# Block-wise search of the early gates, separate buffers for the last router step, a new work list, and the expert stage written once per arm of the branch

## The chip, the cores and the metric

The kernel runs on one core of a Trainium2 chip. The metric is the device time of one execution in microseconds (us), as a median over runs. The core's engines are TensorE (PE, with its weight loads shown as PEld), VectorE (DVE), ScalarE (ACT), GpSimd (POOL) and SyncE (SP). Each works through its own instructions in the order in which they stand, and they wait for each other through semaphores. SP does no arithmetic here; it issues the bulk transfers.

## The reference

A gated linear recurrence over time gives 20224 tokens of 256 numbers, and a mixture of eight experts with a capacity of 80 tokens each works on them. The `x` of the second part is the `h` of the first for four sequences of S = 5056 steps, `gate_w` is the softmax value of the chosen expert. Only the tokens with the highest gates of each expert get an output; all other rows of the output are zero.

```python
log_a = c * sig_r * np.log(np.clip(a_base, 1e-06, 1.0 - 1e-06))[None, None, :]
a_t = np.exp(log_a)
norm = np.sqrt(np.maximum(1.0 - a_t * a_t, 1e-06))
x_gated = norm * sig_i * x
for t in range(S):
    h = a_t[:, t] * h + x_gated[:, t]
...
logits = x @ w_gate
expert_idx = np.argmax(logits, axis=1)
...
for e in range(E):
    tok_idx = np.where(expert_idx == e)[0]
    if len(tok_idx) > capacity:
        keep = np.argpartition(-gate_w[tok_idx], capacity)[:capacity]
        tok_idx = tok_idx[keep]
    h = np.maximum(x[tok_idx] @ w1[e], 0.0)
    out[tok_idx] = gate_w[tok_idx, None] * (h @ w2[e])
```

## The kernel before

**Stage one, the recurrence and the router.** The tokens are cut into 40 units of 512 (the last has 256). For each unit SP loads `r`, `i` and `x` (`load`, L116) into slots of one big tile `Y`; the table `SLOTS` says which. PE transposes `r` (L124), ACT takes its tanh (L126) and the decay `a` (`decay`, L138), POOL squares `a` (`square`, L141), ACT takes a root (`root`, L144) and the tanh of `i` (`i_tanh`, L148). POOL (`u` in the list, L152 and L153) or DVE (`v`, L155) multiplies by `x`, PE transposes the product (L160), DVE applies the norm (`normed`, L163) and runs the recurrence as a scan (`scan`, L171). Some steps take two units at once (`e0.2` is the decay of units 0 and 1). Four finished units make a group. `logits` (L233) multiplies a group by the router's weights into the PSUM tile `pl`, and ten short steps (`stages`) turn two groups into gates: copy (L237), turn by PE (L241), maximum (L252, L253), exp (L258), first maximum (L262 to L264), sum on POOL (L269 to L272), reciprocal (L275), gate (L278), turn back (L283), store into `rows` (L287). There is one `pl` and one `lg` for all steps. `rows` then holds, on each of 128 partitions (16 token classes by 8 experts), the gates of 1264 tokens.

**What sets the order.** `ORDER` is a list of tokens, written out by hand, which fixes the order on ACT, PE, DVE and POOL. SP's order is left to the scheduler. `Z` is one zero fill of the output (256 tokens, 256 KB, L218), of which 79 are needed; fills that the list doesn't hold come after it.

**Selection.** `early_top` (`T`, L292 to L297) searches the first eight groups (1024 columns of `rows`) for the 16 largest per partition after the last scan, while the last router step runs. `top16` then searches those 16 and the last 240 columns together (256 columns). From there DVE, POOL, ACT and PE work out each candidate's rank among the partitions of its expert (`others`, `columns`, `place`, `parts`) and pick the 80 places per expert with matmuls into `sel`, copied to `chosen` (L429). Fourteen candidates per partition are enough in the usual case; if they are not for some partition, `flag` is positive, and `general` (L431 to L473) does it with 80.

**The branch.** PE and DVE load `flag` (L474) and compare (L476). `general` lies right behind the branch, some 480 instructions on DVE and 86 on PE. A hint for the branch is issued on both engines. The program's common rest lies behind `general`; ACT, POOL and SP go to it without looking at `flag`.

**Expert stage.** PE turns `chosen` into columns (L483), DVE makes them integers (L486), and ACT, POOL and DVE each load some columns of an expert into registers (`fetch`, L499) and copy those tokens (L505, L506) into `XG`. PE runs both layers (`products`, L520 and L522), DVE and ACT the relu, DVE the weighting (L530), POOL the scatter (L533). SP loads the weights (L320, L323) of experts 0 and 1 ahead of the last 34 fills, and those of a later expert when its buffers are free. L588 is the program's end, with its barrier.

Of the kernel before, what the change touches and what calls it, by code (L numbers as in the profile page):

```python
# [24 lines left out]
STEPS = ((0, 1), (2, 3), (4, 5), (6, 7), (8, 9))  # L25
SLOTS = dict(r=(1, 2, 3, 4, 5, 10, 14, 16, 21, 22, 13, 24, 29, 31, 33, 27, 37, 38, 41, 21, 22, 35, 44, 45, 46, 30, 40, 48, 31, 33, 49, 43, 36, 46, 47, 44, 49, 43, 42, 47),
             i=(6, 8, 9, 19, 20, 9, 19, 27, 30, 20, 32, 34, 18, 19, 23, 20, 40, 34, 43, 32, 36, 24, 27, 33, 42, 32, 36, 47, 34, 44, 32, 41, 40, 48, 42, 45, 37, 46, 45, 48),
             x=(11, 13, 15, 8, 11, 23, 25, 15, 26, 28, 35, 36, 30, 25, 26, 18, 42, 28, 47, 29, 48, 25, 26, 43, 28, 38, 41, 29, 42, 45, 38, 34, 35, 41, 38, 40, 48, 41, 40, 44),
             a=(0, 7, 12, 17, 18, 6, 7, 8, 12, 9, 11, 17, 14, 15, 16, 19, 23, 17, 20, 31, 49, 34, 23, 37, 24, 25, 27, 35, 28, 37, 30, 31, 32, 33, 34, 35, 36, 38, 41, 39))
# [50 lines left out]
def moe_kernel(ctx, tc, x, r_gate, i_gate, a_param, w_gate, w1, w2, out, capacity=80):  # L80
# [142 lines left out]
    def width(g): return min(512, (N - 2048 * g) // 4)  # L223
    def logits(g):

        s = plan.step_of[g]; k = g - plan.steps[s][0]; last = g == plan.steps[s][-1]
# [366 lines left out]
```

## Time and profile before

| | us |
|---|---|
| median of 3 runs | 332.15 (331.56 to 332.41) |
| the profiled execution, its own time | 329.29 |
| its span in the trace | 327.5 |

Of the span the engines are busy for 68% (PE and DVE) and 71% (ACT and POOL). The last scan ends at 225.4 us. The first matmul of the expert stage starts at 264.65 us, and the rest of the span is the expert stage. Busy times and waits are read per stretch, since the three stages have different limits. A line's rows name what it writes and reads (out<-in), the shape, and the number of instructions.

### The profile page before, as it was taken

The page shows a single profiled execution, that of the slowest core. Times are in us where ns is not written, and L with a number is a line of the kernel's source. Part 1 is how long each engine was busy: PE and PEld are TensorE (multiplying, and loading weights), DVE is VectorE, ACT ScalarE, POOL GpSimd, SP SyncE. Part 2 cuts the span into 40 slices and gives each one's busy share as a digit, 9 for nine tenths or more (in the row PEclk, how much of TensorE's full clock was granted, in tenths as well). Part 3 has the DMA queues.
Part 4 walks back from the last instruction along what each step waited for, and adds up shares of the span by engine and source line. Part 5 has one row for each costly group of instructions (what it writes and reads, how often), then busy time and mean ns, then how long its engine had stood idle before and what let it go on. Part 6 is the DMA issues. An engine that isn't in the chain of part 4 may idle for free. (4 is left out here: it accounts for less than half of the span.)

```text
span 327.5 us, 5668 instructions
## 1 busy us (share of the span) xinstructions
PE 222.6 (68%) x1400; PEld 169.1 (52%) x1400; DVE 222.7 (68%) x515; ACT 231.2 (71%) x454; POOL 231.5 (71%) x358
## 2 busy tenths in 40 slices
PE   3663838496669855798644776348253668999994
PEld 3562833255565343754523326222142558999994
DVE  1047978968579993998659796799684174466611
ACT  6999999989969999689659998891131063453500
POOL 2494999789699999799996989981253167453712
PEclk9957678578579995599975797957757675999999
DMA  7999999999987479896996879999999942999940
GB/s 251 409 404 345 385 412 410 409 370 393 366 327 234 162 260 372 274 309 220 313 366 215 277 208 355 392 374 296 370 375 375 335 165 67 301 353 336 343 149 20
DMA packets 52532, 100.70 MB, mean 307 GB/s; under 512 B 4368, under 2 KB 32912, under 8 KB 52496
## 3 DMA queue, kind: packets, MB, share of 16 engines
q1 hardware_dynamic: 52112, 99.64, 86.0%
q0 software_dynamic: 384, 0.66, 0.6%
q8 instruction: 13, 0.21, 0.3%
q14 instruction: 23, 0.19, 0.2%
HBM read 78.91 MB, written 21.36 MB: 306 GB/s over the span
## 5 line engine op out<-in xcount | busy, mean ns | idle before, releaser
L171 DVE TENSOR_TENSOR_SCAN Y<-Y,pu 128x512 f32<-128x512 f32 (+4 forms) x86 | 97.5, 1169 | 0.4
L160 PE MATMUL pu<-ident,Y 128*128 128x128 f32 x316 | 61.2, 334 | 44.9 <-DVE Y L171 33.6
L141 POOL TENSOR_TENSOR Y<-Y 128x1024 f32<-128x1024 f32 (+2 forms) x29 | 75.2, 2608 | 16.4 <-ACT Y L138 15.9
L160 PEld LDWEIGHTS pu<-ident,Y 128*128 128x128 f32 x316 | 44.4, 172 | 68.3 <-issue 46.3
L153 POOL TENSOR_TENSOR Y<-Y 128x1024 f32<-128x1024 f32 (+2 forms) x25 | 72.9, 2916 | 2.2 <-POOL Y L152 0.2
L124 PE MATMUL pr<-ident,Y 128*128 128x128 f32 x316 | 55.9, 341 | 26.9 <-DMA Y<-in_r_gate_dram 19.0
L124 PEld LDWEIGHTS pr<-ident,Y 128*128 128x128 f32 x316 | 49.1, 181 | 32.4 <-ACT Y L126 14.1
L163 DVE SCALAR_TENSOR_TENSOR pu<-Y,pu 128x512 f32<-128x512 f32 (+1 forms) x80 | 51.2, 676 | 16.5 <-ACT Y L144 11.7
L138 ACT ACTIVATE Y<-Y,tiny 128x512 f32<-128x512 f32 (+2 forms) x58 | 52.4, 961 | 3.0 <-POOL Y L271 2.4
L520 PE MATMUL ph<-Y 128*128 128x80 f32 x256 | 45.7, 273 | 4.4 <-DMA out_dram<-Y 3.0
L522 PE MATMUL po<-Y,rows 128*80 128x128 f32 x256 | 48.3, 282 | 0.0
L148 ACT ACTIVATE Y<-Y 128x1024 f32<-128x1024 f32 (+2 forms) x29 | 38.7, 1359 | 7.8 <-DMA Y<-in_i_gate_dram 7.6
L126 ACT ACTIVATE Y<-pr 128x1024 f32<-128x1024 f32 (+1 forms) x40 | 39.1, 1005 | 7.1 <-PE pr L124 7.1
L520 PEld LDWEIGHTS ph<-Y 128*128 128x128 f32 x256 | 40.6, 206 | 5.0 <-POOL Y L506 3.4
L505 ACT COPY Y<-Y 128x2 f32 x224 | 22.8, 191 | 26.2 <-issue 23.7
L506 POOL COPY Y<-Y 128x2 f32 x192 | 24.3, 200 | 24.0 <-issue 16.1
L152 POOL TENSOR_SCALAR Y<-Y 128x1024 f32<-128x1024 f32 (+2 forms) x25 | 33.8, 1352 | 9.7 <-ACT Y L148 7.3
L233 PE MATMUL pl<-Y 128*32 128x512 f32 (+2 forms) x176 | 37.3, 986 | 2.0 <-ACT rows L287 2.0
L144 ACT ACTIVATE Y<-Y 128x1024 f32<-128x1024 f32 (+2 forms) x32 | 38.0, 1248 | 0.4 <-POOL Y L141 0.3
L522 PEld LDWEIGHTS po<-Y,rows 128*80 128x80 f32 x256 | 29.8, 158 | 0.0
L506 DVE COPY Y<-Y 128x2 f32 x224 | 24.7, 178 | 7.2 <-issue 7.0
L155 DVE SCALAR_TENSOR_TENSOR Y<-Y 128x1024 f32<-128x1024 f32 x9 | 18.0, 2002 | 17.0 <-ACT Y L148 14.8
(131 smaller groups left out, 159.5 us busy)
## 6 DMA issues: line engine op xcount, KB each, us to landing
out_dram<-Y SPq DMA_DIRECT2D x79, 256.0 KB, 4.7
Y<-in_r_gate_dram SPq DMA_DIRECT2D x39, 512.0 KB, 6.3
Y<-in_i_gate_dram SPq DMA_DIRECT2D x39, 512.0 KB, 6.8
Y<-in_x_dram SPq DMA_DIRECT2D x39, 512.0 KB, 5.8
Y<-in_moe_w_dram SPq DMA_DIRECT2D x32, 512.0 KB, 5.0
Y<-in_r_gate_dram SPq DMA_DIRECT2D x1, 256.0 KB, 7.6
Y<-in_x_dram SPq DMA_DIRECT2D x1, 256.0 KB, 7.4
Y<-in_i_gate_dram SPq DMA_DIRECT2D x1, 256.0 KB, 5.2
```

What stands on the lines that cost most here:

```text
L124: nc.tensor.transpose(pr[:, h, b:nb * P:nb], rr[:, b, h * P:(h + 1) * P], ident)
L126: nc.scalar.activation(rslot(u), prs.pop(u)[:, :, :ntok(u)], AF.Tanh, scale=0.5)
L138: nc.scalar.activation(a[:, :, h], z[:, :, h], AF.Exp, scale=L[:, h:h + 1], bias=L[:, h:h + 1])
L141: nc.gpsimd.tensor_tensor(pair('r', u, m), a, a, op=ALU.mult)
L148: nc.scalar.activation(i, i, AF.Tanh, scale=0.5)
L153: nc.gpsimd.tensor_tensor(v, i, v, op=ALU.mult)
L160: nc.tensor.transpose(pu[:, b:nb * P:nb], tmb('x', u)[:, b, h * P:(h + 1) * P], ident)
L163: nc.vector.scalar_tensor_tensor(pu, rslot(u)[:, h], 0.5e-3, pu, op0=ALU.max, op1=ALU.mult)
L171: nc.vector.tensor_tensor_scan(y[:, s0:s1], a[:, s0:s1], q[:, s0:s1], init, op0=ALU.mult, op1=ALU.add)
L506: else: eng.tensor_copy(dst, src)
L520: nc.tensor.matmul(ph[:, c % (FC // 2)], w1v(e1)[:, h, c * P:c * P + P], XG[:, e1, h], start=(h == 0), stop=(h == 1))
L522: nc.tensor.matmul(po[:, h, :P], h2T[:, c], w2v(e2)[:, c, h * P:h * P + P], start=(c == 0), stop=(c == FC - 1))
```

## The change

- **Early search by blocks.** `T` is gone. `P0` to `P3` (`cell_top`) each search 256 columns of `rows` for the eight largest, once these are stored, in the midst of stage one. `M0` to `M2` (`merge`) find the 16 largest of these 32 (DVE) and their columns (DVE, then POOL with a product and halving sums). The eighth of each block, in `eighth`, guards the result: `full` is zero for a candidate that isn't above it, and `fl` counts the candidates that are both out of reach of the capacity and above it, so that `flag` stays zero only if the blocks' eight were enough.
- **Router.** The last two groups are steps of their own: `STEPS` is now `((0, 1), (2, 3), (4, 5), (6, 7), (8,), (9,))`. The last step has its own PSUM tile (a buffer of `ps_r`), its own slot of `Y` in place of `lg`, and its own small columns. Its logits come in two parts: `Ga` for three units, `Gb` for the last; its sum and its gate are on DVE.
- **Work list.** `SLOTS` and `ORDER` are new in every row. Units with the product on DVE are 11 (before 9), on POOL 29 (before 31); pairs are 10, 10, 6 and 10 for decay, square, root and tanh of `i` (before 11, 11, 8 and 11). The weights of experts 0 and 1 (`W0` to `W7`) are in the list. Of the fills 63 are in the list (before 45).
- **Branch.** All five engines load `flag` and compare. The usual arm, a whole copy of the expert stage, stands right behind the comparison; the other arm holds `general` and a second copy. The hints are gone. At its end the usual arm jumps over the other: 975 instructions on DVE, 474 on ACT, 418 on POOL, 390 on PE, 48 on SP.

```diff
-STEPS = ((0, 1), (2, 3), (4, 5), (6, 7), (8, 9))
+STEPS = ((0, 1), (2, 3), (4, 5), (6, 7), (8,), (9,))
...
+    s39.1 xg38.0 W3 R4.0 Tu39.0 xg38.1 R4.1 y38.0 Z W4 y38.1 Tu39.1 Z R4.2 Ga Z xg39.0 R4.3 xg39.1 y39.0 Z y39.1 W5 R4.4 R4.5 Gb Ca M0 W6 R5.0 R5.1
+    W7 R5.2 M1 Z R4.6 R5.3 R5.4 Z Z R5.5 R4.7 R5.6 M2 R4.8 Z R5.7 R5.8 Z R4.9 R5.9
...
+    def logits_first():
+        st['pl', LAST_STEP] = ps_r.tile([P, 2, C], F32, name="pr")[:, 0]
+        spread(LAST, list(range(4 * LAST, NU - 1)))
+    def logits_last(): spread(LAST, [NU - 1])
+    lgs = [lg] * LAST_STEP + [Y[:, NU + 9, 0]]
...
+        if s == LAST_STEP:
+            nc.vector.tensor_reduce(out=total[:n, NR:2 * NR], in_=ex9(n), op=ALU.add, axis=AX.X)
+            return
...
-    def early_top():
-        top16(rows[:, :NE], rows[:, NE:NE + K1], eidx, rows[:, :NE])
-        nc.vector.tensor_copy(ecol, eidx)
+    def cell_top(s):
+        src, c = rows[:, 2 * P * s:2 * P * s + 2 * P], slice(8 * s, 8 * s + 8)
+        nc.vector.max(cell[:, c], src)
+        nc.vector.max_index(cidx[:, c].bitcast(U32), cell[:, c], src)
+    def merge(n):
+        if n == 0:
+            nc.vector.tensor_reduce(out=eighth, in_=cell[:, 7:NC:8], op=ALU.max, axis=AX.X)
+            top16(cell, rows[:, NE:NE + K1], pos.bitcast(U32), cell)
+            nc.vector.tensor_tensor(where, pos.bitcast(U32).unsqueeze(2).broadcast_to([P, K1, NC]), nth.unsqueeze(1).broadcast_to([P, K1, NC]), op=ALU.is_equal)
+        pool = nc.gpsimd
+        if n == 1:
+            pool.tensor_copy(cidx, cidx.bitcast(U32))
+            by8 = cidx.rearrange("p (s k) -> p s k", k=8)
+            pool.tensor_tensor(by8, by8, cell0.unsqueeze(2).broadcast_to([P, 4, 8]), op=ALU.add)
+            pool.tensor_tensor(where, where, cidx.unsqueeze(1).broadcast_to([P, K1, NC]), op=ALU.mult)
+        if n == 2:
+            w = NC // 2
+            while w:
+                pool.tensor_tensor(ecol if w == 1 else where[:, :, :w], where[:, :, 0] if w == 1 else where[:, :, :w],
+                                   where[:, :, 1] if w == 1 else where[:, :, w:2 * w], op=ALU.add)
+                w //= 2
...
-    nc.vector.tensor_scalar(fl, rk[:, K - 1:K], float(CAP), None, op0=ALU.is_lt)
+    nc.vector.scalar_tensor_tensor(lt[:, :K], rk[:, :K], float(CAP), full[:, :K], op0=ALU.is_lt, op1=ALU.mult)
+    nc.vector.tensor_reduce(out=fl, in_=lt[:, :K], op=ALU.add, axis=AX.X)
...
-    _, fv = nc.values_load_multi_w_load_instructions(flag, engines=[E_.PE, E_.DVE], min_val=0, max_val=P,
-    with tc.If(fv[0] > 0, label="many"):
-        general(KG)
+    _, fv = nc.values_load_multi_w_load_instructions(flag, engines=[E_.PE, E_.DVE, E_.Activation, E_.Pool, E_.SP], min_val=0, max_val=P,
+    with tc.If(fv[0] < 1) as usual:
+        experts("u")
+    with usual.Else():
+        gstack = ExitStack()
+        general(KG, gstack.enter_context(tc.tile_pool(name="ps_gen", bufs=1, space=bass.MemoryType.PSUM)))
+        gstack.close()
+        experts("g")
```

On DVE, from the last scan to the last router step's gate. Before, `rows` is searched (L292 to L297) between the scan and the router step (L252 on):

```order
L171 SCALAR_TENSOR_TENSOR Y<-Y,pu 128x256 x2
L292 MAX rows<-rows 128x8
L293 MAX_INDEX tiny<-rows 128x8
L294 MATCH_REPLACE rows<-rows 128x1024
L292 MAX rows<-rows 128x8
L293 MAX_INDEX tiny<-rows 128x8
L297 CAST tiny<-tiny 128x16
L252 TENSOR_REDUCE Y<-pl 128x32
L253 TENSOR_TENSOR pl<-pl,Y 128x16x16
L262 SCALAR_TENSOR_TENSOR pl<-pl,tiny 128x16x16
```

After, in the new kernel's lines, where L283 to L285 end the step of group 8, L330 to L333 are the merge, and L268 begins the last step:

```order
L172 SCALAR_TENSOR_TENSOR Y<-Y,pu 128x256 x2
L283 SCALAR_TENSOR_TENSOR pl<-pl,tiny 128x16x8
L385 TENSOR_TENSOR lg<-lg,ident 48x16
L284 TENSOR_REDUCE Y<-pl 128x16
L285 TENSOR_TENSOR lg<-pl,Y 128x128
L330 TENSOR_REDUCE Y<-Y 128x1
L312 MAX rows<-Y 128x8
L313 MAX_INDEX Y<-rows,Y 128x8
L314 MATCH_REPLACE Y<-rows,Y 128x32
L312 MAX rows<-Y 128x8
L313 MAX_INDEX Y<-rows,Y 128x8
L333 TENSOR_TENSOR Y<-Y 128x512
```

The search over 1024 columns has left this place, and one over 32 columns with a comparison of 512 elements stands there. On POOL, from the last product of stage one on, the rows before are the sum, the gate and two constants:

```order
L153 TENSOR_TENSOR Y<-Y 128x512
L269 TENSOR_TENSOR lg<-lg 128x32x4
L270 TENSOR_TENSOR lg<-lg 128x32x2
L271 TENSOR_TENSOR Y<-lg 128x32
L272 TENSOR_SCALAR Y<-Y 128x32
L278 TENSOR_TENSOR lg<-lg,Y 128x16x2x8
L331 IOTA lg 128x128
L334 IOTA lg 128x80
```

After, L336 to L339 and L343 are the merge, L299 is the gate of group 8, and L378 makes the constant that DVE's L379 reads:

```order
L336 CAST tiny<-tiny 128x32
L338 TENSOR_TENSOR tiny<-tiny,Y 128x32
L339 TENSOR_TENSOR Y<-Y,tiny 128x512
L299 TENSOR_TENSOR lg<-lg,Y 128x128
L343 TENSOR_TENSOR Y<-Y 128x16x16
L343 TENSOR_TENSOR Y<-Y 128x16x8
L378 IOTA lg 128x128
L343 TENSOR_TENSOR Y<-Y 128x16x4
L343 TENSOR_TENSOR Y<-Y 128x16x2
L343 TENSOR_TENSOR tiny<-Y 128x16
```

The merge's products have come in front of the gate and of the constant. On SP, around the last loads of stage one, before:

```order
L116 DMA Y<-in_x_dram 128x512
L116 DMA Y<-in_i_gate_dram 128x512
L218 DMA out_dram<-Y 256x1x256 x23
L320 DMA Y<-in_moe_w_dram 128x2x512 x4
L323 DMA Y<-in_moe_w_dram 128x4x256 x4
L218 DMA out_dram<-Y 256x1x256 x8
L476 UNCONDITIONAL_BRANCH
L218 DMA out_dram<-Y 256x1x256 x26
```

After:

```order
L117 DMA Y<-in_r_gate_dram 128x512
L221 DMA out_dram<-Y 256x1x256 x5
L350 DMA Y<-in_moe_w_dram 128x2x512 x4
L221 DMA out_dram<-Y 256x1x256
L353 DMA Y<-in_moe_w_dram 128x4x256
L221 DMA out_dram<-Y 256x1x256 x3
L353 DMA Y<-in_moe_w_dram 128x4x256 x3
L221 DMA out_dram<-Y 256x1x256 x21
L522 TENSOR_LOAD lg
L615 COMPARE_AND_BRANCH
```

Behind the last load 30 fills are left (before 57), so 49 stand ahead of it (before 22); behind the last weights of experts 0 and 1 there are 21 (before 34).

## Rows read from the trace of the kernel before

**Rows 1.** The page's first part: busy time, share of the span and instructions of each engine.

```profile
PE 222.6 (68%) x1400; PEld 169.1 (52%) x1400; DVE 222.7 (68%) x515; ACT 231.2 (71%) x454; POOL 231.5 (71%) x358
```

**Rows 2.** The view by stretches, for stage one from 100 us on: stretch and length, busy us of PE, PEld, DVE, ACT and POOL with their instructions, granted TensorE clock, mean busy share of the 16 DMA engines, GB/s.

```profile
100.00:120.00 20.00, 16.97 (x110) 9.20 (x108) 19.49 (x23) 19.73 (x19) 19.83 (x8) 1.00 0.58 189
120.00:140.00 20.00, 12.04 (x52) 9.98 (x53) 14.54 (x21) 16.58 (x19) 17.91 (x12) 0.59 0.96 330
140.00:160.00 20.00, 17.04 (x110) 9.52 (x109) 16.21 (x18) 18.34 (x18) 19.68 (x9) 0.98 0.80 280
160.00:180.00 20.00, 9.36 (x51) 6.56 (x50) 16.14 (x24) 14.40 (x17) 16.55 (x13) 0.70 0.83 287
180.00:200.00 20.00, 14.17 (x77) 6.53 (x77) 17.47 (x19) 19.27 (x22) 18.71 (x12) 0.84 0.82 265
200.00:220.00 20.00, 10.01 (x55) 7.63 (x53) 15.14 (x21) 17.54 (x21) 17.33 (x15) 0.76 1.05 374
```

**Rows 3.** The view of waits, whole span: engine and line, what it waited for, us in total, times, longest us.

```profile
ACT Y L148 <- DMA Y<-in_i_gate_dram: 7.6, 3, 5.0
...
ACT Y L126 <- PE pr L124: 7.1, 7, 2.4
```

**Rows 4.** The view of instruction groups with shapes kept apart, from 0 to 226 us: count, busy us, mean ns of one, idle time before.

```profile
L153 POOL TENSOR_TENSOR Y<-Y 128x1024 f32<-128x1024 f32 x18 | 44.4, 2464 | 1.5
...
L138 ACT ACTIVATE Y<-Y,tiny 128x1024 f32<-128x1024 f32 x22 | 26.0, 1232 | 2.5 <-POOL Y L271 2.4
L138 ACT ACTIVATE Y<-Y,tiny 128x512 f32<-128x512 f32 x34 | 25.6, 807 | 0.5 <-DVE pu L163 0.3 <-POOL Y L153 0.2
L144 ACT ACTIVATE Y<-Y 128x1024 f32<-128x1024 f32 x23 | 23.1, 1047 | 0.1
L148 ACT ACTIVATE Y<-Y 128x2048 f32<-128x2048 f32 x11 | 21.0, 1905 | 0.1
L152 POOL TENSOR_SCALAR Y<-Y 128x1024 f32<-128x1024 f32 x18 | 20.8, 1155 | 7.3 <-ACT Y L148 7.3
L155 DVE SCALAR_TENSOR_TENSOR Y<-Y 128x1024 f32<-128x1024 f32 x9 | 18.0, 2002 | 17.0 <-ACT Y L148 14.8 <-DMA Y<-in_x_dram 2.2
L148 ACT ACTIVATE Y<-Y 128x1024 f32<-128x1024 f32 x17 | 17.7, 1049 | 7.7 <-DMA Y<-in_i_gate_dram 7.6
L144 ACT ACTIVATE Y<-Y 128x2048 f32<-128x2048 f32 x8 | 15.1, 1903 | 0.0
```

**Rows 5.** The timeline from the last scan to the search of 256 columns, and three later instructions of like kind: start us, us, engine and line, operation, out<-in, shape and count.

```profile
224.00 1.38 DVE L171 TENSOR_TENSOR_SCAN Y<-Y,pu 128x256 f32<-128x256 f32 x2
...
225.29 1.20 DVE L292 MAX8 rows<-rows 128x8 f32<-128x1024 f32 x1
...
231.86 0.42 DVE L252 TENSOR_REDUCE Y<-pl 128x32 f32<-128x256 f32 x1
...
233.33 0.45 POOL L269 TENSOR_TENSOR lg<-lg 128x128 f32<-128x128 f32 x1 [11.41 <-ACT lg L258]
...
235.81 0.62 POOL L278 TENSOR_TENSOR lg<-lg,Y 128x256 f32<-128x256 f32 x1 [1.03 <-DVE Y L275]
...
237.04 0.23 POOL L331 IOTA lg<- 128x128 int32 x1 [0.61 <-PE pl L283]
...
237.71 0.42 DVE L292 MAX8 lg<-rows 128x8 f32<-128x256 f32 x1
...
242.46 0.68 POOL L345 TENSOR_TENSOR Y<-Y,tiny 128x256 f32<-128x256 f32 x1
...
247.97 0.15 DVE L414 TENSOR_SCALAR lg<-lg 128x1 f32<-128x1 f32 x1
248.04 0.79 DVE L420 TENSOR_TENSOR Y<-lg 128x560 bf16<-128x560 f32 x1
```

**Rows 6.** The sequencers' load of `flag` (L474) and the branch (L476): engine, operation, count, duration in ns (least/median/most), first and last start in us.

```profile
L474 DVEq TENSOR_LOAD <-lg x1: 879/879/879, 250.5 to 250.5; - x1
...
L476 PEldq EVENT_SEMAPHORE  x1: 51/51/51, 251.2 to 251.2; - x1
L476 DVEq COMPARE_BRANCH  x1: 90/90/90, 251.5 to 251.5; - x1
L476 DVEq EVENT_SEMAPHORE  x1: 21/21/21, 255.9 to 255.9; - x1
```

**Rows 7.** The timeline around the branch, and the expert stage's first matmuls.

```profile
250.37 0.23 DVE L429 COPY lg<-sel 48x80 f32<-48x80 f32 x1 [0.71 <-PE sel L426]
...
255.98 0.43 PE L483 MATMUL pv<-lg 48*8 48x80 f32 x2 [5.72 <-DVEq L476]
...
264.65 5.05 PE L520 MATMUL ph<-Y 128*128 128x80 f32 x32 [3.01 <-DMA out_dram<-Y]
```

**Rows 8.** DVE's loads of columns into registers (L499, 28 registers each, one load per expert): columns as in rows 6. The first starts at 256.8 us.

```profile
L499 DVEq TENSOR_LOAD <-lg x8: 1848/1852/4105, 256.8 to 304.1; - x8
```

**Rows 9.** The timeline of SP's queue: the fills behind the last load of stage one, and those behind the first weights.

```profile
207.41 17.59 SPq L218 DMA_DIRECT2D out_dram<-Y  x23
...
232.37 30.01 SPq L218 DMA_DIRECT2D out_dram<-Y  x34
```

**Rows 10.** POOL's sequencer at the end of the program (L588): its drain, the longest of which begins at 323.5 us, and the barrier's semaphores. Columns as in rows 6.

```profile
L588 POOLq EVENT_SEMAPHORE  x4: 17/17/17, 326.7 to 327.4; - x4
L588 POOLq DRAIN  x3: 40/108/2906, 323.5 to 327.2; - x3
```

More of the change, by code (lines that the diff above doesn't have):

```diff
@@ L94, in moe_kernel @@
     Y = big.tile([P, NU + EXTRA, 2, C], F32, name="Y")
-    tiny = const.tile([P, 58], F32, name="tiny")
+    tiny = const.tile([P, 74], F32, name="tiny")
     ident = const.tile([P, P], F32, name="ident")
@@ L323, in load_w2, with weights @@
         nc.sync.dma_start(w2v(e)[:, c], w2[e].rearrange("(c p) d -> p c d", p=P)[:, c])
-    for e, g in ((0, 0), (0, 1), (1, 0), (1, 1)): load_w1(e, g)
-    for e, g in ((0, 0), (0, 1), (1, 0), (1, 1)): load_w2(e, g)
+    WLOADS = [(load, e, g) for load in (load_w1, load_w2) for e in range(2) for g in range(2)]
+    def weights(w):
+        load, e, g = WLOADS[w]
+        load(e, g)
+    tasks = {'Lr': lambda u: load('r', u, rf), 'Li': lambda u: load('i', u, jf), 'Lx': lambda u: load('x', u, xf),
+             'Tr': r_transposes, 'tr': r_tanh, 'e': decay, 'q': square, 's': root, 'ti': i_tanh, 'u': gated, 'v': gated,
+             'Tu': u_transposes, 'xg': normed, 'y': scan, 'G': logits, 'R': lambda s, k: stages[k](s), 'Ga': logits_first, 'Gb': logits_last, 'Ca': copy_first, 'P': cell_top, 'M': merge, 'W': weights, 'Z': lambda: zero_fill(1)}
+    with tc.manual_schedule(engines={E_.Activation, E_.PE, E_.DVE, E_.Pool}):
+        for n, (kind, *args) in enumerate(plan.order):
+            tasks[kind](*args)
+            if n == GATE_AT: nc.sync.dma_start(wg[:, :, E:2 * E], w_gate.rearrange("(h p) e -> p h e", p=P))
+    mstack.close()
+    CAP = capacity
+    assert 0 < CAP <= 80
+    tstack = ExitStack()
+    ps_t = tstack.enter_context(tc.tile_pool(name="ps_t", bufs=1, space=bass.MemoryType.PSUM))
     zero_fill(-(-N // ZERO_TOKENS))
@@ L454, in general @@
             kw = min(16, K - c0)
[L455 removed]
+            others(cv, c0, kw, bd, vv, ps_t)
             for k in range(K):
@@ L480, in moe_kernel @@
-    tail.__enter__()
-    pc = ps_t.tile([E, CAP], F32, name="pv")
-    nc.tensor.matmul(pc, comb[:3 * V, :E], chosen, start=True, stop=True)
-    col = lg[:E, :CAP].bitcast(I32)
-    nc.vector.tensor_scalar(col, pc, -1.0, 0.0, op0=ALU.add, op1=ALU.max)
-    pt = ps_t.tile([CAP, 2 * E], F32, name="sel")
-    nc.tensor.matmul(pt, chosen, comb[:3 * V], start=True, stop=True)
-    keep_warm(WARM[1])
-    flat = slot(0, NU)
-    XG = scr[:, :E * 2 * CAP].rearrange("p (e h s) -> p e h s", e=E, h=2)
```

336 lines of the change are left out of this document (177 added, 159 removed).

## The prediction

> **What bounds the kernel now.** I read the page's busy times first. No engine is above 71% of the span [rows 1], so the end is set by chains of waits, and each stage has to be read for itself.
>
> In stage one the view by stretches [rows 2] shows ACT and POOL close to full: from 100 to 120 us 19.73 and 19.83 of 20 us, from 180 to 200 us 19.27 and 18.71. ACT's idle time has named causes, among them 7.6 us for loads of `i` and 7.1 us for transposes of `r` [rows 3]. The transfers are not full there: shares of 0.58, 0.96, 0.80, 0.83 and 0.82 between 100 and 200 us leave (0.42 + 0.04 + 0.20 + 0.17 + 0.18) x 20 = 20.2 us of idle queue, and only after 200 us is the share 1.05 [rows 2].
>
> The second stage is one long chain. The last scan ends at 224.00 + 1.38 = 225.38 us. DVE then searches 1024 columns from 225.29 to about 231.8, and only then gets to the last router step (L252 at 231.86); the search over 256 columns starts at 237.71 [rows 5], 12.33 us after the scan. `chosen` is written by 250.60, but PE's next matmul starts at 255.98 [rows 7]. The sequencer view says why: DVE branches at 251.5 and its next event is at 255.9, 4.4 us later, though PE had passed the same branch at 251.2 [rows 6]. Next, the first load of columns into registers takes 4.1 us where its median is 1.85 [rows 8], and the expert stage starts at 264.65 [rows 7]. The change aims at this stretch of 39.3 us; the expert stage behind it does the same work as before.
>
> **Stage one, part by part.** The new list splits pairs on ACT. One pair of decays less and two single units more cost 4 x 0.807 - 2 x 1.232 = 0.76 us; two pairs of roots less, 4 x 1.047 - 2 x 1.903 = 0.38; one pair of tanh less, 2 x 1.049 - 1.905 = 0.19: together 1.3 us on the busiest engine [rows 4]. POOL loses two units, 2 x (1.155 + 2.464) = 7.2 us, and DVE gains them, 2 x 2.00 = 4.0 us [rows 4], and the block searches, eight instructions of about 0.42 (L292 on 256 columns, rows 5), 3.4 us. DVE is at 14.5 to 17.5 of 20 us in most stretches [rows 2], so I count that as hidden under ACT; where DVE is late the scans are late with it. Two router instructions of about 0.25 us now stand on DVE ahead of the last norm, where nothing hides them: 0.5 us. So stage one gets 1.8 us longer. I give no credit for POOL's relief: the idle times of ACT in rows 3 don't name it. Bounds: 5 us shorter, if the list removes a third of ACT's 14.7 us of waits for data [rows 3]; 8 us longer, by the fills (third rival).
>
> **The router's tail.** Let T be the end of the last scan. On DVE now follow three operations on 128 elements, which I put at 0.27 between 0.15 (a tiny one, L414) and 0.42 (256 elements, L252), with a small one of 0.16: 1.0 us. The merge: a reduction and five instructions over 32 columns at 0.2 with their overhead, 1.15 us, and the comparison of 512 elements at 0.75, just under L420's 0.79 for 560. That is T + 2.9. POOL then multiplies 512 elements (1.1 us, above L345's 0.68 for 256), gates group 8 (0.45, as L269), halves twice (0.68 and 0.45) and only then makes the constant (0.23, L331) which DVE's next instruction but three reads: T + 5.9 [all rows 5]. DVE waits there: its own last router step could have been there by T + 4.4. Two small constants at 0.23 and four operations of about 0.27 follow, T + 7.5. From the gate's end to the search before were 237.71 - (235.81 + 0.62) = 1.28 us [rows 5]; with half the columns I take 1.1. So the search over 256 columns starts at T + 8.6 in place of T + 12.33: **3.8 us gained** (5.4 if POOL's merge isn't waited for, 1.8 if every small operation costs what a 256-wide one does).
>
> **The guard.** Four more small DVE instructions up to `chosen`, at 0.15 each [rows 5], two of them where DVE waits for PE anyway: **0.3 us lost** (0 to 0.6).
>
> **The branch.** The usual arm now stands right behind the comparison, so I expect no engine to jump there. The flag's load (0.88 us) and the comparison (0.09) stay [rows 6]. DVE's 4.4 us go: **4.4 us gained** (0 to 4.7; the upper end is PE, past the branch at 251.2 and idle until 255.98, rows 6 and 7). Late next is PE itself, which then needs only `chosen`. The three engines that now also load the flag have nothing queued between it and the loads of columns. SP does: it stands behind its last fills, but what it issues in the arm (weights of expert 2) is first needed after two experts.
>
> **The first load of columns.** It takes 4.1 us at 256.8, while SP still issues fills until 232.37 + 30.01 = 262.4 [rows 8, 9]; loads later, beside weight transfers, take 1.85. That the fills slow it is my reading and not shown. A fill takes 30.01 / 34 = 0.88 us, so 13 fills fewer behind the weights end 11.5 us earlier against T, while the load itself comes 3.8 - 0.3 + 4.4 = 7.9 us earlier: the fills' end moves from 5.6 us after its start to 2.0 us after. I take half of the difference: **1.1 us gained** (0 to 2.25).
>
> **The end.** Every engine now jumps over the second arm when it is done. DVE's jump over 480 instructions cost 4.4 us [rows 6]. POOL is last; its drain begins at 323.5 and ends with the last scatter, and the barrier follows at 326.7 [rows 10]. A jump of 4.4 us from 323.5 would end at 327.9, 1.2 us late; one under 3.2 us is hidden. **0.5 us lost** (0 to 1.3), since the transfers there are nearly idle.
>
> [...]
>
> **Sum.** -3.8 + 0.3 - 4.4 - 1.1 + 0.5 + 1.8 = -6.7 us. The profiled execution took 329.29 us (span 327.5), so its like would take 322.6. The median of the three runs is 332.15, and the difference applied to it gives 325.4.
>
> **Rivals.** [...] (2) *The merge buys nothing*: the search leaves DVE, but POOL's product and halvings take its place as the wait in front of L379, with every operation at the 256-wide price and the rest slow as well; the router's term is 0, 329.2. For it: POOL stands idle there for 11.41 us before, so the work is new on the chain [rows 5]; against: the prices. (3) *Slower: the fills choke the loads.* 27 more fills stand ahead of the last load of stage one. At 17.59 / 23 = 0.76 us each [rows 9] they need 20.6 us of a queue with 20.2 us idle. Two bursts of eight and nine stand ahead of loads; each holds a load back by up to 9 x 0.76 = 6.9 us. If stage one gets 10 us longer in place of 1.8, the time is 333.6. The sign turns when the fills take more than 6.7 + 1.8 = 8.5 us from ACT. Against: the scheduler puts them where SP has no free slot to load into. (4) *Stage one gets shorter*: the list removes 5 us of ACT's waits, and its term is -3.2: 320.4.
>
> **How the numbers follow.** Forecast 325.4 with 0.55 (its own range about 321 to 329); rival 1 0.12, rival 2 0.06, rival 3 0.14, rival 4 0.13. The range from 318.0 to 332.0 leaves out most of rival 3 and the low end of rival 4, and takes in the bounds of the router (+2.0, -1.6), the branch (+4.4) and the load (+1.1, -1.1). A difference of 0.3%, about 1 us, is what a measurement here can tell from none. Faster by more: the forecast, rival 4, and nearly all of rivals 1 and 2, 0.82. Within: the overlaps of rivals 1, 2 and part of 3, 0.05. Slower: rival 3, 0.13.
>
> **What would show it.** In the new trace: from the last scan to the search over 256 columns 8.6 us in place of 12.33, with DVE's constant (L379) waiting for POOL; DVE's next event within 0.5 us of its branch; the first load of columns near 3 us, and near 1.85 if the fills are done by then, 4.1 though they are done if my reading of it is wrong; the drain at the end no more than 1.3 us longer; the last scan between 222 and 230 us. The forecast is wrong if the last scan ends after 233 us, or if an engine still stands for 4 us behind its branch.

## The result: 4% faster, twice the forecast

| | before | changed |
|---|---|---|
| median, us | 332.03 (331.56 to 332.41, 4 runs) | 318.2 (316.55 to 318.73, 4 runs) |
| profiled execution, us (span) | 329.29 (327.5) | 318.39 (316.7) |

The ratio is 0.9576, 95% interval 0.9538 to 0.9613. In the runs below the kernel before was timed 52 times beside other kernels, with medians of 330.26, 330.97, 330.44 and 329.83 us and single times from 326.9 to 333.3; the changed kernel came to 317.48 (ratio 0.9596) and 317.57 (0.9626) in two of them. So the first four runs of before were a little high, and the change is worth some 13 us. The forecast was 325.4, 6.7 us less than 332.15; the median of 318.2 lies just inside the range from 318.0 to 332.0, the two later ones just below it. Runs more than 1.5% above the fastest of their kernel (327.18, 327.63 and 320.61 us below, the second of them the first profiled execution with late fills) are in the medians, but no stage is read from them, and where they shift a comparison the median without them is given.

Three profiled executions of the changed kernel and two of before, stage by stage. Each column is the mean of the stage's length; the last is the forecast's term.

| stage, us | before | changed | difference | forecast |
|---|---|---|---|---|
| start to the end of the last scan | 226.4 (225.4, 227.4) | 224.8 (226.1, 224.6, 223.7) | -1.6 | +1.8 |
| to the search over 256 columns | 12.3 | 8.2 | -4.2 | -3.8 |
| to the end of the copy of `chosen` | 12.8 | 12.8 | 0.0 | +0.3 |
| to PE's next matmul | 5.5 | 0.5 | -5.0 | -4.4 |
| to the first expert matmul | 8.6 | 6.9 | -1.7 | -1.1 |
| to the issue of the last scatter | 58.9 | 57.2 | -1.8 | 0 |
| to the end of the span | 3.7 | 5.0 | +1.3 | +0.5 |
| sum | 328.3 | 315.4 | -12.8 | -6.7 |

The page's first part of the changed kernel, to be held against [rows 1]:

```profile
PE 215.4 (68%) x1404; PEld 162.0 (51%) x1404; DVE 228.1 (72%) x541; ACT 233.5 (74%) x463; POOL 227.9 (72%) x370
```

ACT does 2.3 us more (the count of split pairs had 1.3) and DVE 5.4 more, and yet the kernel is shorter. Three stretches of the view beside [rows 2]:

```profile
100.00:120.00 20.00, 16.95 (x106) 8.95 (x104) 19.38 (x18) 19.80 (x22) 18.30 (x8) 0.99 0.99 350
...
140.00:160.00 20.00, 15.09 (x92) 9.49 (x84) 14.76 (x17) 17.57 (x19) 19.75 (x8) 0.88 0.98 350
...
180.00:200.00 20.00, 13.88 (x84) 7.41 (x76) 17.14 (x21) 17.96 (x20) 18.57 (x12) 0.91 0.93 356
```

The DMA share, next to last, is 0.99, 0.98 and 0.93 where it was 0.58, 0.80 and 0.82: most of the idle time of the queue is gone, as 27 more fills stand ahead of the last load. ACT's waits, beside [rows 3]:

```profile
ACT Y L149 <- DMA Y<-in_i_gate_dram: 4.5, 4, 2.9
...
ACT Y L127 <- PE pr L125: 3.6, 7, 1.2
...
ACT lg L276 <- DVE pl L269: 3.2, 2, 2.5
```

The waits for `i` and for transposes of `r` fell from 14.7 to 8.1 us, though the queue is fuller. A wait for the router's maximum (L269) is new.

DVE from the last scan to the search over 256 columns, beside [rows 5]:

```profile
225.38 0.72 DVE L172 TENSOR_TENSOR_SCAN Y<-Y,pu 128x256 f32<-128x256 f32 x1
...
226.93 0.18 DVE L312 MAX8 rows<-Y 128x8 f32<-128x32 f32 x1
...
228.34 0.69 DVE L333 TENSOR_TENSOR Y<-Y 128x512 f32<-128x512 uint32 x1
...
230.30 0.29 DVE L284 TENSOR_REDUCE Y<-pr 112x16 f32<-112x128 f32 x1
232.07 0.33 DVE L379 TENSOR_SCALAR lg<-lg 128x128 int32<-128x128 int32 x1 [1.48 <-POOL lg L378]
...
234.26 0.43 DVE L312 MAX8 lg<-rows 128x8 f32<-128x256 f32 x1 [0.83 <-ACT rows L307]
```

and POOL in the same stretch:

```profile
229.17 1.09 POOL L339 TENSOR_TENSOR Y<-Y,tiny 128x512 f32<-128x512 f32 x1 [2.58 <-DVE Y L333]
230.22 0.41 POOL L299 TENSOR_TENSOR lg<-lg,Y 128x128 f32<-128x128 f32 x1
230.59 1.26 POOL L343 TENSOR_TENSOR Y<-Y 128x256 f32<-128x256 f32 x2
231.80 0.24 POOL L378 IOTA lg<- 128x128 int32 x1
```

DVE is at its last router step by 230.3 and stands for 1.48 us until POOL, which has the merge ahead of it, makes the constant (L378). The branch and PE behind it, beside [rows 6] and [rows 7], first by the sequencers' comparisons, then by PE's timeline:

```profile
L615 POOLq COMPARE_BRANCH  x2: 40/40/41, 247.5 to 311.7; - x2
L615 PEldq COMPARE_BRANCH  x2: 92/1797/3502, 247.6 to 309.0; - x2
L615 DVEq COMPARE_BRANCH  x2: 51/55/59, 247.8 to 311.1; - x2
```

```profile
247.81 0.42 PE L532 MATMUL pv<-lg 48*8 48x80 f32 x2 [1.06 <-DVE lg L476]
...
254.68 1.54 PE L569 MATMUL ph<-Y 128*128 128x80 f32 x12 [0.21 <-DVE lg L592]
```

No engine stands at the branch: PE's next matmul starts at 247.81. The second time on each of these lines is the jump over the other arm at the end. The loads of columns, beside [rows 8], and SP's fills, beside [rows 9]:

```profile
L548 DVEq TENSOR_LOAD <-lg x8: 1849/1857/1957, 248.7 to 292.2; - x8
```

```profile
211.91 3.63 SPq L221 DMA_DIRECT2D out_dram<-Y  x5
...
228.29 17.80 SPq L221 DMA_DIRECT2D out_dram<-Y  x21
```

The last fill is issued by 246.1, ahead of the first load of columns at 248.7, and none of the eight loads is slow. At the end, beside [rows 10], POOL's and DVE's sequencers:

```profile
L645 DVEq DRAIN  x2: 10/25/40, 314.1 to 316.1; - x2
L645 POOLq EVENT_SEMAPHORE  x4: 17/17/17, 315.9 to 316.6; - x4
L645 POOLq DRAIN  x3: 40/107/1262, 314.3 to 316.4; - x3
```

### The profile page after: what moved, and what is told of

The parts are those of the page before. It is cut to its first block, busy times and chain, and to the rows that moved or that the text cites. A ratio compares the mean times of both kernels' runs of the same rounds, so it can differ in the third digit from the quotient of the medians.

```text
span 316.7 us, 5713 instructions
## 1 busy us (share of the span) xinstructions
PE 215.4 (68%) x1404; PEld 162.0 (51%) x1404; DVE 228.1 (72%) x541; ACT 233.5 (74%) x463; POOL 227.9 (72%) x370
## 5 line engine op out<-in xcount | busy, mean ns | idle before, releaser
L142 POOL TENSOR_TENSOR Y<-Y 128x1024 f32<-128x1024 f32 (+2 forms) x30 | 74.2, 2487 | 26.0 <-ACT Y L139 23.6
L161 PE MATMUL pu<-ident,Y 128*128 128x128 f32 x316 | 56.4, 319 | 38.5 <-DVE Y L172 23.3
L125 PE MATMUL pr<-ident,Y 128*128 128x128 f32 x316 | 53.7, 329 | 31.5 <-DMA Y<-in_r_gate_dram 26.9
L161 PEld LDWEIGHTS pu<-ident,Y 128*128 128x128 f32 x316 | 41.9, 163 | 63.3 <-issue 25.2
L154 POOL TENSOR_TENSOR Y<-Y 128x1024 f32<-128x1024 f32 (+2 forms) x25 | 68.6, 2745 | 7.2 <-DMA Y<-in_x_dram 5.2
L125 PEld LDWEIGHTS pr<-ident,Y 128*128 128x128 f32 x316 | 46.4, 174 | 35.5 <-issue 23.5
L569 PE MATMUL ph<-Y 128*128 128x80 f32 x256 | 43.6, 262 | 2.2 <-DVE Y L555 2.0
L569 PEld LDWEIGHTS ph<-Y 128*128 128x128 f32 x256 | 38.6, 196 | 2.7 <-issue 2.7
L156 DVE SCALAR_TENSOR_TENSOR Y<-Y 128x1024 f32<-128x1024 f32 x11 | 23.4, 2130 | 18.7 <-ACT Y L149 12.8
L231 PE MATMUL pl<-Y 128*32 128x512 f32 x144 | 34.2, 1079 | 0.8 <-ACT rows L307 0.8
L153 POOL TENSOR_SCALAR Y<-Y 128x1024 f32<-128x1024 f32 (+2 forms) x25 | 32.1, 1284 | 1.3 <-ACT Y L149 1.1
```

The source lines that it names most:

```text
L125: nc.tensor.transpose(pr[:, h, b:nb * P:nb], rr[:, b, h * P:(h + 1) * P], ident)
L142: nc.gpsimd.tensor_tensor(pair('r', u, m), a, a, op=ALU.mult)
L154: nc.gpsimd.tensor_tensor(v, i, v, op=ALU.mult)
L161: nc.tensor.transpose(pu[:, b:nb * P:nb], tmb('x', u)[:, b, h * P:(h + 1) * P], ident)
L569: nc.tensor.matmul(ph[:, c % (FC // 2)], w1v(e1)[:, h, c * P:c * P + P], XG[:, e1, h], start=(h == 0), stop=(h == 1))
```

## The experiments

**The kernel before, again.** No edit.

> The kernel before, unchanged, once more. Its profiled execution took 329.29 us while its three timed runs had a median of 332.15. Theory: this was chance of one execution, and another one lies between 329 and 333 us with the difference in one of two places: stage one (last scan at 225.4 in the first) or the stall behind the branch (4.4 us). Rival: executions of this kernel taken with a profile are always some 3 us shorter than the others; then this one is at 329.3 again, and the profiled executions of both kernels can't be compared with medians. Timed ratio 1.000 +- 0.002.

Measured: 330.73 us (329.05 to 332.97, 10 runs), ratio 1.0003 (0.9959 to 1.0047); the profiled execution took 330.80, with the last scan at 227.4. So nothing here says that a profile shortens the kernel. The first one, 329.29, was low and the first three timed runs high, and single executions of this kernel spread over 4 us and more.

**The branch alone.** The experts in both arms, five engines loading the flag, in the kernel before:

```diff
-    _, fv = nc.values_load_multi_w_load_instructions(flag, engines=[E_.PE, E_.DVE], ...)
-    with tc.If(fv[0] > 0, label="many"):
-        general(KG)
+    _, fv = nc.values_load_multi_w_load_instructions(flag, engines=[E_.PE, E_.DVE, E_.Activation, E_.Pool, E_.SP], ...)
+    with tc.If(fv[0] < 1) as usual:
+        experts("u")
+    with usual.Else():
+        general(KG, ...); experts("g")
```

> The kernel before with the branch of the changed kernel and nothing else: the usual expert stage stands right behind the comparison, the other search and a second expert stage behind it, five engines load the flag. Computation unchanged. Theory: from `chosen` to the first expert matmul the 4.4 us stall of DVE goes and PE's L483 starts within 1.5 us of `chosen`; the fills still run until about 262 us, so the first load of columns keeps its 4.1 us if the fills slow it; 332.0 - 4.4 + 0.5 = about 328. Rival: it is the jump and not the fills that slows the first load of columns; then it takes 1.85 us here, and the time is near 326.

Measured: 328.95 us (10 runs), ratio 0.9947 (0.9915 to 0.998): 1.3 us or so in place of 4. The stall is gone (PE's matmul 0.40 us behind `chosen`, 5.4 to 5.6 before). It is given back: the expert stage now starts further inside the fills, which SP issues until 265.4. Not only the first load of columns is slow but the second too, on DVE 4.51 and 5.35 us, and PE waits for both:

```profile
261.31 5.87 PE L518 MATMUL ph<-Y 128*128 128x80 f32 x32 [3.85 <-DVE lg L540]
271.19 0.69 PE L518 MATMUL ph<-Y 128*128 128x80 f32 x2 [4.00 <-DVE Y L504]
```

From the first expert matmul to the end it takes 67.2 us in place of 62.6; 1.4 us of that are behind the last scatter's issue, where the jump over the second arm now is.

**The branch taken back.** The changed kernel with the branch of before, its hints, and one expert stage:

```diff
-    with tc.If(fv[0] < 1) as usual:
-        experts("u")
-    with usual.Else():
-        general(KG, ...); experts("g")
+    with tc.If(fv[0] > 0, label="many"):
+        general(KG, ...)
+    experts("u")
```

> The changed kernel with the branch of the kernel before: the other search stands behind the comparison, the usual arm jumps over it, PE and DVE load the flag, the hints are back, one expert stage, no jump at the end. Computation unchanged. Theory: DVE stands for 4.4 us behind its branch again. The fills end at about 246, before the first load of columns, so that load stays at 1.85 us if the fills slow it: time about 318.2 + 4.4 - 0.5 = 322. Rival: the jump slows the load; it takes 4.1 us, and the time is about 324.5.

Measured: 319.82 us (4 runs), ratio 0.9691 (0.9632 to 0.9749). The load stays at 1.87 us although DVE jumps ahead of it, which is against the rival. The stall is back but shorter: PE's matmul 3.65 us behind `chosen`, against 0.5 in the changed kernel and 5.5 before. And the end is shorter: 3.73 us from the last scatter's issue to the end of the span. So in the changed kernel the branch is worth some 2 us, 3.1 gained at the start less 1.3 lost at the end.

**13 fills more.** Behind the weights, 13 blocks are filled a second time:

```diff
     zero_fill(-(-N // ZERO_TOKENS))
+    nz[0] = 0
+    zero_fill(13)
```

> The changed kernel with 13 fills more behind the weights (13 blocks of the output are filled twice, so the work is more and the result the same); at 0.88 us each the fills end 11.4 us later, at about 257.5, nine microseconds after the first load of columns begins. Theory (fills slow the load): that load takes 4.1 us in place of 1.86, time 318.2 + 2.25 = 320.5. Rival (jump): the load stays at 1.86, the time at 318.2 or up to 1 us more if the later weights are missed.

Measured: 321.01 us (4 runs; 320.12 without 327.18), ratio 0.973 (0.9665 to 0.9794). The profiled execution is the lowest, 317.26 us, since its last scan happened to end at 222.4; the time alone would not decide. In its trace the first load of columns is slow again, though nothing of the branch was changed:

```profile
L550 ACTq TENSOR_LOAD <-lg x8: 1718/1742/4129, 244.7 to 292.1; - x8
L550 POOLq TENSOR_LOAD <-lg x8: 1544/1574/3672, 244.7 to 291.8; - x8
L550 DVEq TENSOR_LOAD <-lg x8: 1851/1856/4382, 244.7 to 291.5; - x8
```

From PE's restart to the first expert matmul it takes 9.0 us in place of 6.9. With the run before this settles it: the fills slow the loads of registers (4.38 us on DVE), the jump doesn't (1.87).

**The changed kernel, again**, beside the next three.

> The changed kernel, unchanged, timed beside the others of this call. Theory: the kernel before spreads from 328.5 to 333.3 us over 19 runs with a median of 330.3, so the 332.0 of four runs was high; the changed kernel stays at 318.2 and the ratio is 318.2 / 330.3 = 0.963. Rival: the four runs were typical on their chip, the ratio is 0.957 again.

Measured: 317.48 us (4 runs), ratio 0.9596 (0.9544 to 0.9647).

**One search.** The block searches and the merge out, the search over 1024 columns back behind the last scan:

```diff
-    ... P0 ... P1 ... P2 ... P3 ... M0 ... M1 ... M2 ...
+    ... y39.1 T ...
+    def early_top():
+        nc.vector.memset(eighth, -1.0)
+        top16(rows[:, :NE], rows[:, NE:NE + K1], cidx[:, :K1].bitcast(U32), rows[:, :NE])
+        nc.vector.tensor_copy(ecol, cidx[:, :K1].bitcast(U32))
```

> The changed kernel with the block searches and the merge taken out and the one search over 1024 columns put back behind the last scan, as in the kernel before (the guard then always agrees); buffers of the last router step, list, fills and branch stay changed. Result unchanged. Theory: the search (6.5 us on DVE, seven instructions on 1024 columns) comes back on the path, the merge (4 us) goes, and DVE's wait of 1.5 us for POOL goes too; from the last scan to the search over 256 columns 8.15 - 1.5 - 2.2 + 6.5 = about 11, the last scan 0 to 3 us earlier, time 318.2 + 2 = 320. Rival: the buffers for the last step brought all of the gain; then the step stays near 8.5 us and the time at or below 318.

Measured: 320.63 us (4 runs), ratio 0.9695 (0.965 to 0.974). From the last scan to the search over 256 columns 11.06 us, between 8.15 and 12.33: the new last router step (its own buffers, logits in two parts, sum and gate on DVE) brought 1.3 us, searching by blocks 2.9.

**The fills late**, in the changed list where before has them (22, 23 and 34), run twice:

```diff
-    R0.6 xg14.0 Z xg14.1 R0.7 e19.1
+    R0.6 xg14.0 xg14.1 R0.7 e19.1
...
-    e39.1 q38.1 xg37.1 W0 s38.1
+    e39.1 q38.1 xg37.1 Z Z Z Z Z Z Z Z Z Z Z Z Z Z W0 s38.1
```

(27 tokens Z are taken out in this way, 14 put in front of W0; the other 13 fills follow the weights.)

> The changed kernel with its fills moved back to where the kernel before has them: 22 ahead of the last load of stage one, 23 between it and the weights and among them, 34 behind (before: the same; changed: 49, 9, 21). Computation unchanged. Theory: the earlier fills are what makes the branch pay; with 34 behind the weights the first three loads of columns take 4 us and more again, the weights of expert 2 come late, and from `chosen` to the end it takes about 7 us longer as in the kernel with the branch alone (76.8 against 69.6), while stage one, whose queue had idle time, ends where it did or up to 2 us earlier: 318.2 + 6 = 324. Rival: the fills ahead of the loads slow stage one by as much as they save behind it; then the last scan ends 5 us earlier and the time is 318 to 319.

> The changed kernel with its fills late (22, 23 and 34 as in the kernel before) once more, for a profile of an undisturbed execution. Theory: last scan at 224.8 +- 1.5 as with the early fills, so the new order of work and not the fills brings the earlier scan; the first load of columns over 4 us; from the first expert matmul to the end 66 to 67 us, since the weights of expert 2 stand behind the fills; time 322.5. Rival: last scan at 222 or below, that is the early fills do cost stage one 3 us.

Measured: 322.53 us (4 runs, 322.26 without 327.63; ratio 0.9735, 0.9686 to 0.9783) and 322.18 us (6 runs, ratio 0.9765, 0.9721 to 0.9809), so some 4 to 5 us are lost. In the second profile the last scan ends at 224.6, where it ended with early fills. Behind it, stage by stage: the first load of columns 4.51 us on DVE, the second 4.24, the first expert matmul 9.3 us behind PE's restart in place of 6.9, from there to the end 65.6 in place of 62.2.

```profile
L548 DVEq TENSOR_LOAD <-lg x8: 1849/1859/4510, 247.2 to 296.3; - x8
```

**The constant early.** `se`, made by POOL at L378 in the middle of its halvings, gets its own place in `scr` and is made ahead of the merge; DVE's two operations on it move to where it waits for ACT's copy:

```diff
+    se = scr[:, 320:320 + P]
+    def same_expert(se):
+        nc.gpsimd.iota(se.bitcast(I32), pattern=[[1, P]], base=P, channel_multiplier=-1)
+    def same_expert2(se):
+        nc.vector.tensor_scalar(se.bitcast(I32), se.bitcast(I32), E - 1, None, op0=ALU.bitwise_and)
+        nc.vector.tensor_scalar(se, se.bitcast(I32), 0.0, None, op0=ALU.is_equal)
...
         if n == 0:
...
+            same_expert(se)
...
+        if n == 3: same_expert2(se)
...
-    se = lg[:, :P]; iot = lg[:, P:P + 80]
-    nc.gpsimd.iota(se.bitcast(I32), pattern=[[1, P]], base=P, channel_multiplier=-1)
...
-    ... R5.7 R5.8 Z R4.9 R5.9
+    ... R5.7 R5.8 M3 Z R4.9 R5.9
```

> The changed kernel, and the constant that DVE waits 1.48 us for (made by POOL between its halvings, read by DVE two instructions later) gets a place of its own and is made ahead of the merge; DVE's two operations on it move to where it waits for the copy of the last rows. Computation unchanged. Theory: DVE's wait goes, the last step and the search come 1.5 us earlier, 318.2 - 1.5 = 316.7. Rival: POOL's halvings end last anyway and the search's result waits for them, or the copy of step five's rows holds the search: less than 0.5 us gained.

> The changed kernel with the constant made ahead of the merge, as run before (316.8 against 317.5, with spreads of 3 us): its trace had the search 1.43 us earlier behind the last scan. Theory: 1.4 us are left in the time, 316.4 against 317.8. Rival: they are given back, and the two are within 0.5 us.

Measured: 316.78 us (6 runs, ratio 0.9591, 0.9554 to 0.9628) and 316.5 us (6 runs, ratio 0.9592, 0.9556 to 0.9627), beside 317.48 and 317.57 for the changed kernel. In the traces DVE's wait is gone and the search starts 6.72 and 6.70 us behind the last scan in place of 8.15. DVE's timeline in the second run:

```profile
230.54 0.29 DVE L284 TENSOR_REDUCE Y<-pr 112x16 f32<-112x128 f32 x1
230.87 0.29 DVE L285 TENSOR_TENSOR Y<-pr,Y 112x128 f32<-112x128 f32 x1
...
232.41 0.23 DVE L332 TENSOR_SCALAR Y<-Y 128x128 f32<-128x128 int32 x1
233.06 0.43 DVE L312 MAX8 lg<-rows 128x8 f32<-128x256 f32 x1 [0.42 <-ACT rows L307]
```

Both medians lie below those of the changed kernel timed beside them, by 0.7 us each (the second against 317.19, without 320.61); the intervals of the ratios overlap, so the 1.4 us are shown in the stage and not in the time.

**The changed kernel a third time**, beside the last run above and the two parts that follow.

> The changed kernel once more, in the same call as the two parts above and the one below, so that they stand against it: 317.5 to 318.2.

Measured: 317.57 us (6 runs), ratio 0.9626 (0.9584 to 0.9668).

**The list alone.** SLOTS and ORDER of the changed kernel in the kernel before, without the tokens for block searches (P, M), weights (W) and the split last step (Ga, Gb, Ca, R4, R5), and without 9 of the last Z; router step four and the search stand where before has them. The end of the list:

```diff
-    ... y39.0 Z y39.1 W5 R4.4 R4.5 Gb Ca M0 W6 R5.0 R5.1
-    ...
+    ... y39.0 y39.1 T G9 R4.0 R4.1 R4.2 R4.3 R4.4 R4.5 R4.6 R4.7 R4.8 R4.9
```

> The kernel before with the changed kernel's list of stage one and its fills (54 of 79 fills ahead of the weights of experts 0 and 1, 25 behind; before 45 and 34, most of them later), and nothing else: router steps in five, one search over 1024 columns behind the last scan, old branch. Computation unchanged. My sum has the last scan 0.5 us later with this part alone in stage one's list, plus 1.3 us of split pairs, that is later by 0 to 2 us, and 1.1 us back at the first load of columns: no change, 330 to 331. Theory after the first two calls: the list ends the last scan 1 to 2 us earlier (mean of six executions with it 224.8 us, of three without 226.5), the branch costs 3 us in place of 4.8 because the fills are done, and the first loads of columns take 1.9 us in place of 4: 330.6 - 1.5 - 1.9 - 1.8 = 325.4.

Measured: 324.13 us (4 runs), ratio 0.9821 (0.9785 to 0.9858). The list with its fills brings 6.3 us by itself. The last scan ends at 224.8; the stall is 3.84 us from `chosen` to PE; the first load of columns takes 1.86; from PE's matmul to the first expert matmul 6.43 (8.6 before), from there to the end 61.5 (62.6 before). DVE's branch, which took from 251.5 to 255.9 in [rows 6]:

```profile
L478 DVEq COMPARE_BRANCH  x1: 90/90/90, 250.4 to 250.4; - x1
L478 DVEq EVENT_SEMAPHORE  x1: 21/21/21, 253.6 to 253.6; - x1
```

That is 3.2 us in place of 4.4 for the same jump. What differs here, and in the run with the branch taken back (SP's last fill there is issued by 244.3 us, its next transfer at 258.9), is what the queues carry meanwhile: the stretch of the stall in the view by stretches (columns as in [rows 2]), first in this kernel, then in the kernel before:

```profile
249.70:254.20 4.50, 0.49 (x3) 0.23 (x4) 0.19 (x2) 0.00 (x0) 0.00 (x0) 0.57 0.02 5
```

```profile
250.50:256.00 5.50, 0.02 (x1) 0.02 (x2) 0.10 (x1) 0.00 (x0) 0.00 (x0) 0.50 1.01 346
```

**The list and the branch.** The edit above and the branch of the second experiment together.

> The kernel before with the changed kernel's list, its fills and its branch, without block searches and without the own buffers of the last router step. Computation unchanged. Theory (the branch pays only where the fills are done): 330.6 - 1.5 (last scan) - 4.8 (stall) - 1.8 (loads) = 322.5, and a little more than the kernel with one search and own buffers (320.6). Rival (parts add up as timed alone, branch -1.3): the list's time minus 1.3.

Measured: 322.4 us (4 runs), ratio 0.9766 (0.9715 to 0.9818): 1.7 us less than the list alone, against 4.8 expected. The stall of 3.84 us goes to 0.22, and the end gets 0.4 us longer here; the rest of what is missing is no more than the intervals of the two ratios allow. The new last router step (320.63) and the block searches (317.6) make up the way to the changed kernel, so the parts in this order are 6.3, 1.7, 1.8 and 3.1 us, with medians side by side that were not all taken beside each other.

**The fills early in the old list.** 27 more behind the same numbers of loads as in the changed list, 14 fewer in front of the weights:

```diff
-    xg39.1 Z y39.0 Z y39.1 Z T Z G9 Z Z Z R4.0 Z R4.1 Z Z Z Z R4.2 Z R4.3 Z R4.4
+    xg39.1 y39.0 y39.1 T G9 R4.0 R4.1 R4.2 R4.3 R4.4
```

(The 27 go in behind the 71st to the 96th load of stage one.)

> The kernel before with its own list, its branch and its search; only the fills stand as early as in the changed list (27 more behind the same numbers of loads as there, 14 fewer in front of the weights, so 21 behind them in place of 34). Computation unchanged. Theory (the fills' places bring most of the list's 6.3 us): stall behind the branch 3.8 in place of 5.5, first load of columns 1.9, expert stage from its first matmul 61.5 in place of 62.6, together 4.7; last scan unchanged at 225 to 227.5: 330.5 - 4.7 = 325.8. Rival (the fills choke the loads of a list that was not made for them): the last scan comes 3 us later or more, and the time is above 328.

Measured: 326.84 us (4 runs), ratio 0.9897 (0.9842 to 0.9951), some 3 us gained. The last scan at 227.5 is not earlier and hardly later. The last fill is issued by 255.5, so fills still run in the stall, which starts at 252.5 and keeps its 5.4 us, and the load behind it, at 258.7, takes 1.87; from PE's matmul 6.43 and 61.6 us, as with the list alone. So this is what the places of the fills are worth without a shorter stall.

## Why the forecast fell short

**The step that failed is the list's.** "Stage one, part by part" added up ACT's split pairs and DVE's searches and came to +1.8 us, with the fills as a danger to the loads; the only gain that the fills were given was 1.1 us at the first load of columns. Together the list was to cost 0.7 us. Alone it gains 6.3: 1.6 us at the last scan, 1.6 in the stall, 2.2 from there to the first expert matmul and 1.1 behind it, by its trace. That difference of 7 us is about as large as the whole miss, though the stall's 1.6 are in the branch's term as well. In the table the miss of 6.1 us is 3.4 in stage one (-1.6 in place of +1.8) and 1.8 in the expert stage, which had no term; the other terms are off by 0.3 to 0.8 each.

Two things are in it, and the last pairs of runs part them. *The places of the fills.* 3 us in the old list, 4 to 5 in the new one, and no cost in stage one: the last scan ends at 224.6 with late fills and at 223.7 to 226.1 with early ones; 227.5 with early fills in the old list and 225.4 to 227.4 with late ones. The queue's 20 idle us that the prediction counted were there to be used, and the third rival (the fills choke the loads by 10 us) didn't come; a cost of 1 or 2 us would be lost in this spread. *The order of the work.* In the eleven executions with the new list that are read here, the last scan ends at 222.4 to 226.4, mean 224.8; in the four with the old one, at 225.4 to 227.5, mean 226.7. That is 1.9 us earlier in place of 1.8 later. In the four traces with the old list ACT waits 7.6 to 11.3 us for `i`, in the eleven with the new one 2.5 to 4.5. That is what rival 4 said; in the changed kernel new waits (L276 for DVE's L269, 3.2 us) take a part back. The waits go along with the earlier scan; that they are its cause was not tested by itself. The split pairs, counted on an engine that had 14.7 us of such waits, cost nothing that shows in the end of the scan.

**The first load of columns.** The reading that the fills slow it was right, and is now shown: 13 fills more bring the slow load back (4.4 us on DVE), a jump in front of it doesn't (1.87 with the branch taken back, all eight loads at 1.85 to 2.00 with the list alone). The term was two thirds of the true one (-1.1 against -1.7), since I took the fills to end inside the load; they ended ahead of it. What I missed is that the same fills reach the engine behind it: in before PE runs the expert stage at a granted clock of 0.92 in two executions, in the changed kernel, with the fills out of its way, at 0.95 to 0.97, and its 512 matmuls there are busy 54.4 us in place of 56.9 to 57.3. The fills alone do this: 13 more in the changed kernel give 0.91 and 57.4 us, late ones 0.89 and 58.4, early ones in the old list 0.97 and 54.4. The last scatter is issued 1.8 us earlier against the first expert matmul, where I had put nothing.

**The branch.** From `chosen` to PE -5.0 us against the forecast's -4.4, and five engines with a flag to load cost nothing, as said; PE's matmul is 0.5 us behind `chosen`, so rival 1, by which an engine still stands at its branch, is out. But the price belongs to its surroundings: the same edit brings 1.3 us alone, because the fills then slow two loads of columns, and 1.7 where the fills are early, because the stall between `chosen` and PE from which it takes is then 3.65 to 3.84 us and not 5.4 to 5.6, and the end gives a part back.

**The end.** The jump over the second arm was to cost 0.5 us, at most 1.3. From the last scatter's issue to the end of the span it takes 3.70 to 3.73 us in all five executions without a second arm, and 4.1 to 5.75, mean 5.0, in ten with one: 1.3 us, the end of the range. The size came out, the mechanism didn't. The sum had POOL's jump outlast the scatter. In the changed kernel that jump is over at 314.3 us, where POOL's drain begins, and the drain then lasts until 315.6, 0.3 us after the scatter has landed. It is the scatter that lands later: the last one 2.3 us behind its issue in the five executions, 3.1 to 4.3 in eight of the ten. In the other two it takes 2.3 as well, and there the end is only 0.4 and 0.6 us longer. Why it lands later beside the jumps was not tested. For all eight scatters of a profile, first before, then changed:

```profile
DMA to landing us min/median/max: 2.3/4.5/5.3
```

```profile
DMA to landing us min/median/max: 3.3/4.4/5.1
```

The last scatter of the changed kernel is issued at 311.89; with the branch taken back at 314.31, and there the span ends 3.73 us later in place of 4.77:

```profile
311.89 0.91 POOL L582 DMA_INDIRECT out_dram<-Y,lg  x1 [2.40 <-DVE Y L579]
```

```profile
314.31 0.91 POOL L586 DMA_INDIRECT out_dram<-Y,lg  x1 [2.40 <-DVE Y L583]
```

The 0.5 us rested on a jump being shorter where the transfers are nearly idle (DMA share 0.09 in before, from 323.5 to 326.7), which was an estimate; DVE's jump over `general` has since taken 3.2 us beside a share of 0.02 and 4.4 beside 1.01. The jumps at the end show on two engines, beside a share of 0.13 to 0.16: DVE, done with its work at 311.6, has its next event behind the comparison at 311.1 only at 314.1 (over 975 instructions), and POOL, behind 311.7 with its last scatter busy until 312.8, at 314.3 (over 418). PE's comparison at 309.0 lasts 3.5 us, but its own last matmuls run until 311.1, so no more than 1.4 us of it come after PE's work:

```profile
307.21 3.88 PE L571 MATMUL po<-Y,rows 128*80 128x128 f32 x34
```

**The router's tail** went as forecast: 8.15 us against 8.6, with DVE's wait for L378 where it was said to be; the merge does not eat the gain (rival 2), but 1.4 us of POOL's order could still be had. **The guard** costs nothing that shows (12.8 us either way).

**The base.** 2.9 us were added to go from one profiled execution to the median of three. 52 more timed runs put the medians at 329.8 to 331.0, some 1.1 us above the first profiled execution. With that the forecast would have been 323.7, and still 5.5 us high.

## What to carry to other kernels

A bulk write that nobody waits for was not free here where it stood (3 us in the old list, 4 to 5 in the new): put it where the queue idles, and look behind the last load for what it slows, here a register load (4.1 us in place of 1.87), a jump (4.4 in place of 3.2) and the start of the next stage (9.3 us behind PE's restart in place of 6.9). Two edits that meet in one stretch are worth neither the sum nor the price of each alone, so time the one without the other before either is credited. Counting instructions on the busiest engine says little while it waits 15 us for data; and a base of three runs can be off by more than the terms that are being added up.

## What the runs showed of the hardware

A load of 28 registers takes DVE 1.85 to 1.87 us with idle queues (DMA share 0.00) and 4.1 us beside the fills in before (share 1.02), up to 5.35 us in the run with the branch alone. It is not the share alone: beside weight transfers at a share of 0.91 to 1.10 the last four loads of the changed kernel take 1.85 to 1.96 us. A single register, the flag, takes 0.79 and 0.88 us beside the fills in before (share 1.08) and 0.68 to 0.96 us in the changed kernel, where the fills are still moving (share 0.99 from 245.7 to 247.7 us). The same jump on DVE takes 3.2 us with a DMA share of 0.02 and 4.4 beside the fills with one of 1.01. The load of 28 registers and the jump are no transfers that the program issues, and both took longer beside the fills. Executions of one kernel spread over 1% here (329.05 to 332.97 us in ten of before), much of it ahead of the end of the last scan (222.4 to 226.4 us with the new list), so a gain of 1 us shows in a stage of the trace and not in ten timed runs.
